# Reordering the first loads of a squared-ReLU MLP: x on one queue, w1 behind the activation table load

## The chip, the cores and the metric

The kernel runs on one NeuronCore of one Trainium2 chip. The metric is the device time of one execution in microseconds (us); the time before is the median of nine runs.

The engines are named as in the profile: PE is TensorE's matmul, PEld its weight load, DVE is VectorE, ACT is ScalarE, POOL is GpSimd, SP is SyncE. SPq and ACTq are the instruction queues of SyncE and ScalarE, from which loads are issued.

## The reference

```python
B, S, D, F = 1, 2048, 576, 4608          # x, w1, b1, w2, b2 all bfloat16

h = jnp.einsum("bsd,df->bsf", x, w1) + b1
zero = jnp.zeros_like(h)
r = jnp.where(h > zero, h, zero)
h = r * r
out = jnp.einsum("bsf,fd->bsd", h, w2) + b2
```

Two matrix products with a squared ReLU between them: 2048 rows, 576 columns in, 4608 hidden, 576 out.

## The kernel before

The 2048 rows are worked on in four blocks of 512. For each block the kernel forms h transposed (hidden units on partitions, rows along the free axis): ScalarE applies ReLU with the bias (L169), VectorE squares (L170), and the second product reads the result (L253 and L272). All of w1 and w2 is loaded once and stays in SBUF.

The first product needs x transposed. For blocks 1 to 3 a transposing DMA delivers it. For block 0 [...]the block is loaded plainly as four x tiles of 128 rows (`load_x`, L72), transposed by TensorE against an identity (`x_transpose`, L146, five 128x128 transposes per tile) and copied out of PSUM by VectorE (L151, L153) and ScalarE (L152) in two halves of 256 rows (`x_copies`). Afterwards VectorE makes a second arrangement of the same data (`dup_windows`, L115 and L116).

The first 512 hidden units of block 0 are computed in the order "k outer": `part(h, k)` does four matmuls of 256 rows (L217) with the k-th chunk of 128 rows of w1 (`w1n`, four chunks, `load_w1n`, L76). The order is k = 0 to 3 for the first half of the rows, then k = 0 to 3 for the second, with the bias transposed in between (`make_b1T`, L159). A last pair of matmuls (L196, L198) uses the remaining 64 rows of w1, which are loaded twice, into the upper and the lower half of the partitions (`w1n8`, `load_w1n8`, L79). Then `a_rows` goes through the rest of w1 (`w1_h`, `w_h` in the profile, L82) in blocks of two times nine matmuls (L181, L183).

While the first loads are on their way TensorE runs warm-up matmuls on a constant (`WARM`, L63). ScalarE needs its activation table before its first activation; a dummy activation (L97, into a tile of its own) brings that load in early.

Order: nearly every operation is wrapped in `keep`, which holds it in program order on its engine. The loads are split by hand: SyncE issues x tiles 0 and 2, w1n chunks 0 and 2, then w1n8 and all of w1_h; ScalarE issues x tiles 1 and 3 and w1n chunks 1 and 3, then runs the table load and the dummy activation, then issues the b1 load (L98). In the compiled program eight completion semaphores are handed out to the loads in turn, so a load also waits until the load that had its semaphore eight loads before has landed.

```python
WARM = [512] * 6 + [256]
...
load_x(nc.sync, 0)
load_x(nc.scalar, 1)
load_x(nc.sync, 2)
load_x(nc.scalar, 3)
for k in range(NK):
    load_w1n(nc.sync if k % 2 == 0 else nc.scalar, k, k + 1)
```

Of the kernel before, what the change touches and what calls it, by code (L numbers as in the profile page):

```python
# [9 lines left out]
ACT = mybir.ActivationFunctionType  # L10
ALU = mybir.AluOpType
BF16 = mybir.dt.bfloat16
FP32 = mybir.dt.float32
# [4 lines left out]
def kernel(  # L18
# [9 lines left out]
    nc = tc.nc  # L28
    keep = tc.keep_in_program_order
    P = 128  # L30
# [5 lines left out]
    NFT = F // P  # L36
# [8 lines left out]
    RT = SB // P  # L45
# [3 lines left out]
    const = ctx.enter_context(tc.tile_pool(name="const", bufs=1))  # L49
# [8 lines left out]

    wps = ps_h.tile([P, 512], FP32, name="wps", tag="ph")
    ones = nc.const_aps.tensor(1.0, [P, 512], BF16)  # L60
    WARM = [512] * 6 + [256]
    for i, n in enumerate(WARM):
        keep(nc.tensor.matmul(wps[:, 0:n], lhsT=ones[:, 0:P], rhs=ones[:, 0:n], start=True, stop=True))  # L63

    xs = const.tile([P, RT, D], BF16, name="x_sb")
    w1n = wpool.tile([P, NK, GW], BF16, name="w1n")
# [4 lines left out]
    def load_x(eng, rt):  # L71
        keep(eng.dma_start(out=xs[:, rt, :], in_=x2[rt * P:(rt + 1) * P, :]))  # L72

    def load_w1n(eng, k0, k1):
        src = w1[k0 * P:k1 * P, 0:GW].rearrange("(k p) f -> p k f", p=P)
        keep(eng.dma_start(out=w1n[:, k0:k1, :], in_=src))  # L76

    def load_w1n8(eng, h):
        keep(eng.dma_start(out=w1n8[h * H:(h + 1) * H, :], in_=w1[NK * P:D, 0:GW]))  # L79
# [5 lines left out]
    b1_rows = const.tile([P, P], BF16, name="b1_rows")  # L85
    nc.vector.memset(b1_rows[:], 0.0)
    load_x(nc.sync, 0)
    load_x(nc.scalar, 1)
    load_x(nc.sync, 2)
    load_x(nc.scalar, 3)  # L90
    for k in range(NK):
        load_w1n(nc.sync if k % 2 == 0 else nc.scalar, k, k + 1)

    ident = const.tile([P, P], BF16, name="ident")
    make_identity(nc, ident[:])
    warm = const.tile([P, 1], FP32, name="warm")
    keep(nc.scalar.activation(out=warm[:], in_=nc.const_aps.tensor(0.0, [P, 1], FP32), func=ACT.Relu))  # L97
    keep(nc.scalar.dma_start(out=b1_rows[0:NFT, :], in_=b1.rearrange("(ft p) -> ft p", p=P)))  # L98
    for h in range(2):
        load_w1n8(nc.sync, h)  # L100

    E3, O, SPC, E = 0, 1, 5, 6
    LO_W = [O, O + 1, O + 2, O + 3, E, E + 1, E + 2, E3, SPC]
# [240 lines left out]
```

## Time and profile before

| | |
|---|---|
| median of 9 runs | 291.16 us (290.58 to 291.32) |
| profiled execution | 291.12 us, span of its instructions 289.4 us |
| PE busy | 284.8 us (98% of the span), 2027 matmuls |
| DVE busy | 78.6 us (27%) |
| ACT busy | 96.5 us (33%) |
| DMA | 16.59 MB, mean 57 GB/s |

The table reads as follows: TensorE is busy nearly all the time, the other engines a third of it or less, and the DMA engines are busy only in the first quarter of the span. The span runs from the first to the last instruction; the execution's time has 1.7 us around it. Of the start-up the timeline has these numbers: the loads begin to be issued at 0.73 us, the table load starts at 2.61 and takes 1.28, the first transpose starts at 3.58, the first L217 matmul at 6.01.

### The profile page before, as it was taken

How to read it: one execution, taken by the hardware profiler on the slowest of the kernel's cores; microseconds unless marked ns; L12 is line 12 of the kernel's file. 1: busy time of each engine (PE TensorE's matmuls, PEld its weight loads, DVE VectorE, ACT ScalarE, POOL GpSimd, SP SyncE). 2: the span in 40 equal slices, each digit the busy share in tenths (PEclk: the TensorE clock that was granted, in tenths of full speed). 3: DMA queues.
4: the chain of work that ended last, by engine and by line, in shares of the span. 5: the costliest groups of instructions: out<-in, count | busy, mean ns of one | idle time of the engine just before them, and what ended most of it. 6: DMA issues, size and time to landing. Idle time of an engine off the chain costs nothing.

```text
span 289.4 us, 4690 instructions
## 1 busy us (share of the span) xinstructions
PE 284.8 (98%) x2027; PEld 139.2 (48%) x2032; DVE 78.6 (27%) x177; ACT 96.5 (33%) x152; POOL 0.9 (0%) x7
## 2 busy tenths in 40 slices
PE   7999999999999999999999999999999999999996
PEld 4544444444444555555544444444444455555555
DVE  3444554444500200000015444444440001100001
ACT  3566666666500000000027666666670000000000
POOL 0000000000000000000000000000000000000000
PEclk9999999999999999999999999999999999999999
DMA  6999999300001200000000000000000110000000
GB/s 198 233 239 194 315 388 217 78 0 2 0 17 25 49 16 18 16 16 18 16 16 2 1 2 0 2 0 2 0 2 0 36 39 16 16 16 19 31 17 18
DMA packets 31573, 16.59 MB, mean 57 GB/s; under 512 B 15552, under 2 KB 31552, under 8 KB 31552
## 3 DMA queue, kind: packets, MB, share of 16 engines
q1 hardware_dynamic: 30928, 15.72, 21.8%
q10 hardware_dynamic: 624, 0.57, 0.7%
q8 instruction: 16, 0.26, 0.4%
q14 instruction: 5, 0.04, 0.0%
HBM read 11.43 MB, written 2.36 MB: 48 GB/s over the span
## 4 chain that ended last, share of the span: by engine, by line
PE 98%; DVE 0%; issue 0%
PE ph L181 42%; PE po L272 38%; PE pt L253 11%; PE pn L202 4%; PE pn L217 1%; PE wps L63 1%; PE ph L183 1%; PE pn L196 1%; PE tb L146 1%; DVE xTw L151 0%; DVE o_sb L274 0%; DVE xTw L153 0%; PE b1T_ps L159 0%; PE pn L198 0%
## 5 line engine op out<-in xcount | busy, mean ns | idle before, releaser
L183 PE MATMUL ph<-xTw,w_h 64*128 64x512 bf16 x576 | 124.6, 376 | 0.0
L181 PE MATMUL ph<-xTw,w_h 64*128 64x512 bf16 x576 | 124.6, 376 | 0.0
L272 PE MATMUL po<-w_sb,hT 128*128 128x448 bf16 (+2 forms) x612 | 109.4, 341 | 0.0
L169 ACT ACTIVATE r<-ph,b1T 128x512 bf16<-128x512 f32 x128 | 81.1, 685 | 41.6 <-PE ph L183 41.6
L181 PEld LDWEIGHTS <-w_h 64*128 64x128 bf16 x576 | 54.1, 94 | 68.3
L272 PEld LDWEIGHTS <-hT 128*128 128x128 bf16 x612 | 58.5, 98 | 51.0
L170 DVE TENSOR_TENSOR hT<-r 128x512 bf16<-128x512 bf16 x144 | 61.2, 426 | 76.9 <-ACT r L169 76.6
L183 PEld LDWEIGHTS <-w_h 64*128 64x128 bf16 x576 | 54.1, 94 | 0.0
L274 DVE TENSOR_TENSOR o_sb<-po,b_bc 128x448 bf16<-128x448 f32 (+2 forms) x17 | 10.2, 598 | 125.8 <-PE po L272 125.8
L253 PE MATMUL pt<-hT,w_sb 128*128 128x512 bf16 x142 | 31.3, 379 | 0.1
L169 ACT ACTIVATE r<-pn,b1T 128x512 bf16<-128x512 f32 x16 | 10.3, 688 | 62.7 <-PE pn L198 61.3
L253 PEld LDWEIGHTS <-w_sb 128*128 128x128 bf16 x144 | 14.1, 98 | 17.0
L256 ACT ACTIVATE oT<-pt,b2T 128x512 bf16<-128x512 f32 x4 | 2.7, 687 | 28.3 <-PE pt L253 28.3
L202 PE MATMUL pn<-xTw,w1n 128*128 128x512 bf16 x45 | 10.4, 379 | 0.4 <-issue 0.3
L202 PEld LDWEIGHTS <-w1n 128*128 128x128 bf16 x48 | 4.5, 98 | 6.0 <-issue 0.8
L217 PE MATMUL pn<-xTw,w1n 128*128 128x256 bf16 x32 | 3.7, 273 | 0.7 <-DVE xTw L153 0.7
L63 PE MATMUL wps<-const-bfloat16-1.0 128*128 128x512 bf16 (+1 forms) x7 | 2.9, 597 | 0.8 <-PEq L328 0.8
L217 PEld LDWEIGHTS <-w1n 128*128 128x128 bf16 x32 | 3.0, 98 | 1.2 <-DMA w1n<-in_w_dram 0.8
L115 DVE COPY xTw<-xTw 64x2048 bf16<-64x2048 bf16 x4 | 2.8, 690 | 0.5 <-ACT xTw L152 0.4
L116 DVE COPY xTw<-xTw 64x2048 bf16<-64x2048 bf16 x4 | 2.8, 688 | 0.1
L198 PE MATMUL pn<-xTw,w1n 64*128 64x512 bf16 x8 | 2.4, 379 | 0.0
L196 PE MATMUL pn<-xTw,w1n 64*128 64x512 bf16 x8 | 2.4, 379 | 0.0
(21 smaller groups left out, 11.1 us busy)
## 6 DMA issues: line engine op xcount, KB each, us to landing
w_sb<-in_w_dram SPq DMA_DIRECT2D x2, 2592.0 KB, 15.0
w_h<-in_w_dram SPq DMA_DIRECT2D x14, 288.0 KB, 6.8
out_dram<-o_sb SPq DMA_DIRECT2D x15, 112.0 KB, 1.7
w_h<-in_w_dram SPq DMA_DIRECT2D x4, 144.0 KB, 3.2
out_dram<-ot SPq DMA_DIRECT2D x4, 128.0 KB, 2.0
x_sb<-in_x_dram ACTq DMA_DIRECT2D x2, 144.0 KB, 2.9
x_sb<-in_x_dram SPq DMA_DIRECT2D x2, 144.0 KB, 2.8
w1n<-in_w_dram ACTq DMA_DIRECT2D x2, 128.0 KB, 3.9
```

The source lines that it names most:

```text
L63: keep(nc.tensor.matmul(wps[:, 0:n], lhsT=ones[:, 0:P], rhs=ones[:, 0:n], start=True, stop=True))
L146: keep(nc.tensor.transpose(tb[h][bank][:, slot, q * P:(q + 1) * P], xs[:, j, c0:c0 + P], ident[:]))
L169: keep(nc.scalar.activation(out=r[:], in_=bank[:], func=ACT.Relu, bias=b1T[:, ft:ft + 1], scale=1.0))
L170: keep(nc.vector.tensor_tensor(out=hTs[sb][:, ft, :], in0=r[:], in1=r[:], op=ALU.mult))
L181: keep(nc.tensor.matmul(bx[:], lhsT=w1_h[0:H, LO_C[i], jc], rhs=xT[0:H, LO_W[i], :], start=(i == 0), stop=(i == NC - 1)))
L183: keep(nc.tensor.matmul(by[:], lhsT=w1_h[H:P, UP_C[i], jc], rhs=xT[H:P, UP_W[i], :], start=(i == 0), stop=(i == NC - 1)))
L196: keep(nc.tensor.matmul(banks[2 * i][:], lhsT=w1n8[0:H, 2 * i * P:(2 * i + 1) * P], rhs=xT[0:H, SPC, :], start=start, stop=stop, skip_grou ...
L202: keep(nc.tensor.matmul(banks[g][:], lhsT=w1n[:, k, g * P:(g + 1) * P], rhs=xT[:, O + k, :], start=start, stop=stop))
L217: keep(nc.tensor.matmul(banks[g][:, hc], lhsT=w1n[:, k, g * P:(g + 1) * P], rhs=xT[:, O + k, hc], start=(h == 0 and k == 0), stop=False, s ...
L253: keep(nc.tensor.matmul(pt[:], lhsT=w2_sb[:, ft, DM:D], rhs=hT[:, ft, :], start=(i == 0), stop=(i == NFT - 1)))
L272: keep(nc.tensor.matmul(po[:, 0:d1 - d0], lhsT=hT[:, ft, jj * P:(jj + 1) * P], rhs=w2_sb[:, ft, d0:d1], start=(i == 0), stop=(i == NFT - 1)))
L274: keep(nc.vector.tensor_tensor(out=o_sb[:, d0:d1], in0=po[:, 0:d1 - d0], in1=b2_bc[:, d0:d1], op=ALU.add))
```

## The change

Five edits, all in the start-up:

1. The warm-up has 5 x 512 + 384 = 2944 columns instead of 6 x 512 + 256 = 3328.
2. All four x tiles are issued by SyncE, in order 0, 1, 2, 3.
3. The dummy activation moves to the head of ScalarE's queue. It no longer writes a tile of its own but the first column of w1n chunk 0, so the load of that chunk, which overwrites this column, has to wait until the activation has ended. The b1 load follows it on ScalarE's queue.
4. The w1n chunks swap queues: 0 and 2 on ScalarE, 1 and 3 on SyncE behind the x tiles.
5. The two w1n8 loads move from SyncE to ScalarE, behind its w1n chunks. ScalarE's L152 copies (L150 in the changed file) come after them in its queue.

In the compiled order of the changed kernel ScalarE has: table load, activation, b1 load (waits for VectorE's memset), w1n chunk 0 (waits for the activation), w1n chunk 2, first w1n8 half (waits for x tile 1 to land), second w1n8 half (waits for b1 to land), the two copies. SyncE has: x tiles 0 to 3, w1n chunk 1, w1n chunk 3 (waits for x tile 0 to land), then w1_h, of which the first waits for x tile 2, the second for x tile 3, the third for w1n chunk 0. The other engines' orders are unchanged, but for one warm-up matmul less.

```diff
-    WARM = [512] * 6 + [256]
+    WARM = [512] * 5 + [384]
...
     load_x(nc.sync, 0)
-    load_x(nc.scalar, 1)
-    load_x(nc.sync, 2)
-    load_x(nc.scalar, 3)
+    keep(nc.scalar.activation(out=w1n[:, 0, 0:1], in_=nc.const_aps.tensor(0.0, [P, 1], FP32), func=ACT.Relu))
+    keep(nc.scalar.dma_start(out=b1_rows[0:NFT, :], in_=b1.rearrange("(ft p) -> ft p", p=P)))
+    for rt in range(1, RT):
+        load_x(nc.sync, rt)
     for k in range(NK):
-        load_w1n(nc.sync if k % 2 == 0 else nc.scalar, k, k + 1)
+        load_w1n(nc.scalar if k % 2 == 0 else nc.sync, k, k + 1)
+    for h in range(2):
+        load_w1n8(nc.scalar, h)
 
     ident = const.tile([P, P], BF16, name="ident")
     make_identity(nc, ident[:])
-    warm = const.tile([P, 1], FP32, name="warm")
-    keep(nc.scalar.activation(out=warm[:], in_=nc.const_aps.tensor(0.0, [P, 1], FP32), func=ACT.Relu))
-    keep(nc.scalar.dma_start(out=b1_rows[0:NFT, :], in_=b1.rearrange("(ft p) -> ft p", p=P)))
-    for h in range(2):
-        load_w1n8(nc.sync, h)
```

## The prediction

> **What bounds the kernel now.** I read the page first, then the waits of TensorE (PE), then the chain of work over the first microseconds, then the transfers one by one. The page's chain says where the span goes:
>
> ```profile
> PE 98%; DVE 0%; issue 0%
> ```
>
> PE's own waits over the whole span are three lines, and its weight loads' waits five, of which these two are for transfers:
>
> ```profile
> PE wps L63 <- PEq L328: 0.8, 1, 0.8
> PE pn L217 <- DVE xTw L153: 0.7, 1, 0.7
> PE pn L202 <- issue: 0.3, 2, 0.2
> ...
> PEld L217 <- DMA w1n<-in_w_dram: 0.8, 1, 0.8
> PEld L146 <- DMA x_sb<-in_x_dram: 0.8, 2, 0.6
> ```
>
> The reader is to see that all that PE loses to loading lies in the start-up. From the first L217 matmul on, PE is fed to the end. So an edit of the start-up is worth exactly the move of that matmul, as long as nothing behind it runs dry. The chain of the first microseconds (start, length, what):
>
> ```profile
> 0.77 2.93 PE wps L63 x7
> 3.71 0.89 PE tb L146 x10
> 4.62 0.63 PE tb L146 x8
> ...
> 6.01 2.36 PE pn L217 x20
> ```
>
> The first L217 matmul starts at 6.01. PE's wait before it is named DVE (the chain puts L151 and L153 of the second half of x there), but those feed later matmuls; the first needs only the first L151 copy, and its weight load waits for w1n. The entries for that chunk's load on SyncE (start 1.68) and for the loads and the table load on ScalarE:
>
> ```profile
> DMA to landing us min/median/max: 4.3/4.3/4.3
> ...
> 2.61 1.28 ACT L97 ACT_TABLE_LOAD   x1 [2.61 <-issue]
> 3.90 0.20 ACT L97 ACTIVATE warm<-const-float32-0.0 128x1 f32<-128x1 f32 x1
> 4.65 0.56 ACTq L98 DMA_DIRECT2D b_rows<-in_b_dram  x1
> ```
>
> 1.68 + 4.3 = 6.0: chunk 0 of w1n lands just when PE starts. In the same way chunk 1 (ScalarE, 1.64 + 3.7) lands at 5.3, chunk 3 (2.1 + 4.2) at 6.3 and chunk 2 (2.16 + 4.3) at 6.5; x tiles 0 and 1 at 3.5 and 3.3, tile 3 at 4.4, and tile 2 at 4.6, when PE's second batch of transposes starts. Why so late is in the stretches (busy times, then clock, DMA share, GB/s):
>
> ```profile
> 1.60:2.00 0.40, 0.40 (x2) 0.13 (x1) 0.00 (x0) 0.00 (x0) 0.00 (x0) 1.00 0.55 60
> 2.00:2.40 0.40, 0.40 (x2) 0.15 (x1) 0.00 (x0) 0.00 (x0) 0.00 (x0) 1.00 0.74 196
> 2.40:5.20 2.80, 2.78 (x24) 1.71 (x22) 0.68 (x3) 1.49 (x2) 0.00 (x0) 1.00 1.04 338
> ```
>
> From 2.4 to 5.2 the DMA engines are full (share 1.04) at 338 GB/s. Start-up is bound by bytes and by their order, not by issue.
>
> **The change part by part.**
>
> *Bytes.* Four x tiles of 147 KB and four w1n chunks of 131 KB are 1.11 MB before and after. About 0.10 MB has moved by 2.4 (60 and 196 GB/s for 0.4 us each), the other 1.01 MB takes 3.0 us: 5.4, and the last chunk lands about 1 us later (6.5). No reordering moves that last landing. [...] The row agrees on bandwidth (338 GB/s shared by both), but what PE waits for is the first chunk, which landed third of four. L217 runs 20 matmuls in 2.36 us, 0.118 each, so a chunk's four take 0.47, and chunks 1, 2, 3 are needed 0.47, 0.94 and 1.42 after chunk 0. Even with the last at 6.5, PE could start at 5.1 if the last is chunk 3. I take the row: order can give up to 0.9 us.
>
> *x on SyncE alone.* Tiles 0 to 3 are issued 0.42 to 0.44 us apart from 0.73, tile 3 at about 2.1 where it was at 1.2. Alone on the engines, tile 0 is through by about 2.7 and lands at about 3.1 (3.5 before), tiles 1 and 2 follow by 0.44 each (3.5, 3.9 to 4.1). Tile 3 depends on what ScalarE's queue has in flight then.
>
> *Warm-up.* 3328 columns become 2944. Six matmuls start 0.43 apart, so 384 columns are 0.32 us: transposes may start at 3.25 instead of 3.57. Alone this is worth nothing, tile 2 and w1n come later; it only avoids delaying tile 0.
>
> *ScalarE.* The table load moves from 2.61 to 0.73 and ends at about 2.0, the ACTIVATE (now into w1n, which the load of chunk 0 overwrites) at 2.22. The compiled order has the b1 load next, waiting only for the memset (ends 0.93), then chunk 0, waiting for the ACTIVATE, chunk 2, and the two w1n8 halves; the first waits for x tile 1, the second for b1 (completion semaphores are reused after eight loads); behind these are the two L152 copies. Whether b1 is issued while the table load runs is not in the trace. Bounds: at 0.97, then chunk 0 at 2.3; or at 2.25 for 0.56, then chunk 0 at 2.85. I take the first, because nothing that b1 itself waits for is later, and keep both. [...] In the row the ACTIVATE starts 0.01 us behind the load. [...]
>
> *w1n.* ScalarE's first traffic came 1.1 us after its first issue (0.73 to about 1.8), so chunk 0 flows from 3.4, when SyncE's x tile 3 is still to come and tile 2 partly. The queues shared evenly before (tiles 0 and 1 landed 0.2 apart), so chunk 0 takes (2 x 131)/338 = 0.78 us, to 4.2; x tile 3 is through at 4.3 to 4.5 and lands at 4.7 to 4.9. Chunks 1 (SyncE) and 2 (ScalarE) share the next 0.78 us, to about 5.2, and land 0.4 to 0.9 later, as the landings before did: 5.6 to 6.1. Chunk 3 (SyncE, whose semaphore waits for x tile 0, long landed) is through by 5.7 and lands by 6.5.
> PE's first L217 matmul is then the latest of: transposes (tile 3 at 4.8, five at about 0.08: 5.2); chunk 0 (4.7 to 5.1); chunk 1 less 0.47 (5.1 to 5.6); chunk 2 less 0.94 (4.7 to 5.2); chunk 3 less 1.42 (5.1). I take 5.5, chunk 1's upper part, because before the last of a pair's landings came at the late end. With b1 behind the table load (chunk 0 at 2.85) x is clear of w1, tile 3 lands at 4.4, and the same sum gives 5.1 to 5.3.
>
> *What must not become late.* L152 copies: the second w1n8 issue ends at about 4.7 (5.5 with b1 late), the copies at 5.3 and 5.9 (6.1 and 6.7); needed at 6.4 and about 8.5. The dup copies (2 x 0.69) end by 7.4 (8.1), the pair needs them 3.66 after the start, 9.2. w1n8 lands by 7 to 7.5, also needed at 9.2. SyncE's queue is one issue shorter, with the w1n8 halves (0.57 each) gone and tiles 1 and 3 (0.43 each) come: the first w_h waits for x tile 2 and goes at about 4.1 instead of 4.63, later ones keep that lead of 0.3 to 0.6. The tightest w_h was issued at 8.05 and landed 5.2 later, 13.3, for a block that starts at about 14.0; both shift together, so its cover of 0.7 holds. Cost of all these: nothing.
>
> *Sum.* 6.01 - 5.5 = 0.5 us less. The profiled execution took 291.12 us (span 289.4), 0.04 below the median of 291.16. So span 288.9, execution 290.62, median about 290.65, or -0.18%. What a measurement of this kernel can tell from no change is 0.2%, 0.58 us.
>
> **The rivals.**
>
> *More is gained.* b1 waits behind the table load, or landings have the short tail of the x tiles (0.4): PE starts at 5.1 to 5.3, right behind the transposes, time 290.35 (290.2 to 290.5). For it: SyncE alone can keep the engines full. Against: nothing shows a stall of ScalarE's queue behind a table load.
>
> *Slower: the TensorE clock is released later.* The transposes show the step: those of 3.6 to 3.9, then those of 4.6 to 5.1,
>
> ```profile
> L146 PE MATMUL tb<-ident,x_sb x4: 289/314/314, 3.6 to 3.9; 128*128 128x128 bf16 x4
> L146 PE MATMUL tb<-ident,x_sb x10: 219/219/229, 4.6 to 5.1; 128*128 128x128 bf16 x10
> ```
>
> so full speed came at about 4.2, after 3.4 us in which PE had no gap. [...] With the shorter warm-up, gaps of 0.1 to 0.3 us open wherever an x tile lands after 3.25, 3.7 or 4.1. [...] Net of the 0.5: +0.65 to +0.75, median 291.8. It decides as soon as the release is later than about 6.5. Against: x tile 0 should land before 3.25[...].
>
> *Nothing is gained.* Sharing with chunk 0 makes tile 3 land at 5.4, or chunk 1 lands at 6.5[...]: start at 5.9 to 6.5, time 291.05 to 291.65. For it: chunk 0 landed 0.6 after chunk 1 before, though issued together.
>
> **How the numbers follow.** Main case (start 5.3 to 5.8, 290.45 to 290.95) 0.50, of which 0.12 lies below 290.58, that is over 0.2% faster. More gained: 0.27, all faster. Clock slips: 0.14, all slower. Nothing gained: 0.09, of which 0.06 within 0.2% and 0.03 slower. Faster 0.39, within 0.2% 0.44, slower 0.17. The likeliest case gives 290.65, its own range 290.45 to 290.95. The range 290.0 to 291.8 takes in the gain if every landing is early (start 4.9) and reaches the middle of the clock case.
>
> **What would show it.** Right: table load at 0.73; chunk 0's issue at about 2.3 on ScalarE; x tile 0 landing by 3.25; last transposes ending near 5.2; first L217 at 5.5 with its weight load or the second chunk's waiting for w1n; no new wait of PE after it. Wrong: transposes of 314 ns after 4.5, L217 matmuls 0.2 us apart (clock);[...] x tile 3 landing after 5.2 (sharing); PE waiting for L152 or w_h.

## The result, and the profile after

The changed kernel is slower: 291.66 us median (17 runs, 291.31 to 293.34) against 291.01 for the kernel before on the same chips (51 runs), ratio 1.0032, 95% interval 1.0024 to 1.0041. Eleven of the 17 lie within 291.31 to 291.71, three at 293.1 to 293.3; none of the 51 runs before is above 291.64. The forecast was 290.65. Here and below the ratio follows the means of the runs (291.91 against 290.97 here), so it includes the runs near 293, and it leaves out three executions in a slow state: 434.89 us in experiment 4, 303.66 in experiment 7 (its profiled one, at a granted clock of 0.95) and 378.45 of the kernel before.

The profiled execution took 291.71 us (span 289.9). Its chain is no longer TensorE (PE) alone; the page's shares of the span:

```profile
PE 87%; SPq 8%; DMA 3%; issue 1%; DVE 0%
```

The waits of the weight loads (us in total, times, longest) have lost w1n and gained w_h:

```profile
PEld L144 <- DMA x_sb<-in_x_dram: 1.6, 3, 0.8
...
PEld L181 <- DMA w_h<-in_w_dram: 1.1, 2, 0.5
```

TensorE's start-up, as the timeline has it (start, length, idle before and what ended it):

```profile
3.18 1.27 PE L144 MATMUL tb<-ident,x_sb 128*128 128x128 bf16 x10
4.98 0.45 PE L144 MATMUL tb<-ident,x_sb 128*128 128x128 bf16 x5 [0.53 <-DMA x_sb<-in_x_dram]
5.65 0.45 PE L144 MATMUL tb<-ident,x_sb 128*128 128x128 bf16 x5 [0.22 <-DMA x_sb<-in_x_dram]
5.96 2.34 PE L215 MATMUL pn<-xTw,w1n 128*128 128x256 bf16 x20
```

x tile 0 is early as planned, but tiles 2 and 3 come at 4.95 and 5.6, later than the 4.6 and 4.4 of before. The first matmul on w1n (now L215) starts at 5.96 instead of 6.01: nearly nothing gained. The first matmul on w_h starts at 10.04 instead of 10.11. From there to the end of the span it is 279.9 us, where it was 279.3, so in this pair of profiles all of the loss lies behind the start-up. There PE loses time twice, as the chain shows for the second loss (start, length):

```profile
28.91 5.05 DMA w_h<-in_w_dram
34.00 0.39 PE ph L181
```

Both waits are for pieces of w1_h. The other one ends at 14.35: that piece was issued at 8.44 and landed 5.9 later (8.05 and 5.2 before). By the last block of the first stage PE is 0.59 us late (its matmuls start at 73.61, before at 73.02), and stays so to the end.

What had changed for w_h is in the stretches 10 to 18 us (w_h, with a transposing load issued at 17.73 before) and 36 to 44 us (w2), beside 2.4 to 4.0 us (start-up loads). The last two columns are the DMA share and GB/s. Before, then after:

```profile
2.40:4.00 1.60, 1.60 (x9) 0.73 (x8) 0.00 (x0) 1.38 (x2) 0.00 (x0) 1.00 1.04 340
10.00:18.00 8.00, 8.00 (x78) 3.60 (x74) 4.26 (x10) 6.12 (x10) 0.00 (x0) 1.00 1.21 244
36.00:44.00 8.00, 8.00 (x78) 3.60 (x75) 4.07 (x10) 5.29 (x10) 0.00 (x0) 1.00 1.08 388
```

```profile
2.40:4.00 1.60, 1.60 (x11) 1.07 (x10) 0.00 (x0) 0.00 (x0) 0.00 (x0) 1.00 0.94 236
10.00:18.00 8.00, 7.95 (x73) 3.42 (x71) 4.23 (x10) 6.11 (x10) 0.00 (x0) 1.00 1.22 201
36.00:44.00 8.00, 8.00 (x78) 3.62 (x76) 4.23 (x10) 5.30 (x9) 0.23 (x1) 1.00 1.09 345
```

The engines are as full as before in the last two stretches (1.22 and 1.09), but move 18% and 11% less. These loads are issued in the same order from the same queue in both kernels. What differs is their destination. The change dropped the dummy activation's own tile, which took 32 bytes per partition, and everything allocated behind it moved by as much. In the compiled program w1n, w1_h (the tile of w_h) and w2 start at multiples of 256 bytes of a partition before, and 32 bytes short of one after.

### The profile page after: what moved, and what is told of

It reads as the page before. It is cut to its first block, busy times and chain, and to the rows that moved or that the text cites. A ratio compares the mean times of both kernels' runs of the same rounds, so it can differ in the third digit from the quotient of the medians.

```text
span 289.9 us, 4688 instructions
## 1 busy us (share of the span) xinstructions
PE 285.2 (98%) x2026; PEld 139.2 (48%) x2031; DVE 78.6 (27%) x177; ACT 96.6 (33%) x152; POOL 0.9 (0%) x7
## 4 chain that ended last, share of the span: by engine, by line
PE 87%; SPq 8%; DMA 3%; issue 1%; DVE 0%
PE po L270 38%; PE ph L179 21%; PE ph L181 14%; PE pt L251 11%; SPq L82 5%; PE pn L200 4%; SPq L120 2%; DMA w_h<-in_w_dram 2%; DMA x_sb<-in_x_dram 1%; SPq L121 0%; PE pn L194 0%; SPq L72 0%; PE pn L196 0%; DVE o_sb L272 0%
## 5 line engine op out<-in xcount | busy, mean ns | idle before, releaser
L215 PE MATMUL pn<-xTw,w1n 128*128 128x256 bf16 x32 | 3.7, 272 | 0.0
L215 PEld LDWEIGHTS <-w1n 128*128 128x128 bf16 x32 | 3.0, 98 | 0.3
L144 PE MATMUL tb<-ident,x_sb 128*128 128x128 bf16 x20 | 2.2, 268 | 0.7 <-DMA x_sb<-in_x_dram 0.7
L144 PEld LDWEIGHTS <-x_sb 128*128 128x128 bf16 x20 | 1.7, 121 | 1.7 <-DMA x_sb<-in_x_dram 1.6
```

The lines of the kernel that those rows point to most:

```text
L144: keep(nc.tensor.transpose(tb[h][bank][:, slot, q * P:(q + 1) * P], xs[:, j, c0:c0 + P], ident[:]))
L215: keep(nc.tensor.matmul(banks[g][:, hc], lhsT=w1n[:, k, g * P:(g + 1) * P], rhs=xT[:, O + k, hc], start=(h == 0 and k == 0), stop=False, s ...
```

## The experiments

All ratios are to the kernel before, run on the same chip.

**1. Is it the addresses or the queues?** The changed kernel with the 32 bytes set aside again:

```diff
     make_identity(nc, ident[:])
+    pad = const.tile([P, 1], FP32, name="pad")
```

> The changed kernel, with 32 bytes of SBUF per partition set aside where the dummy activation's own tile lay before, so that w1n, w1_h, w2 and the tiles behind them have their old addresses (multiples of 256) again. Address theory (the change removed a 32-byte tile, everything behind it moved by 32 bytes, and loads into such addresses are slower): w_h moves at about 240 GB/s between 10 and 25 us instead of 198, PE no longer waits for w_h, ratio to the kernel before 0.9995 to 1.000 (the first L215 matmul still starts at 5.9 to 6.0). Queue theory (the first w_h is issued 0.3 us later because its completion semaphore waits for x tile 2, and all of w_h lands late behind it): addresses do nothing, w_h at about 200 GB/s, PE waits about 0.6 us for w_h, ratio 1.003.

Measured: 291.16 us, ratio 1.0013 (1.0002 to 1.0023). Its stretches:

```profile
2.40:4.00 1.60, 1.60 (x11) 0.95 (x10) 0.00 (x0) 0.00 (x0) 0.00 (x0) 1.00 1.00 249
10.00:18.00 8.00, 8.00 (x78) 3.62 (x76) 4.26 (x10) 6.13 (x11) 0.00 (x0) 1.00 1.17 254
36.00:44.00 8.00, 8.00 (x78) 3.60 (x74) 4.05 (x10) 5.30 (x9) 0.00 (x0) 1.00 1.08 387
```

The rates of w_h and w2 are back and no wait for w_h is left. More than half of the loss is gone, not all: two of 22 runs were at 293.08 (without them the mean is 0.06% above the kernel before), and the order of the queues, with good addresses, is still no gain.

**2. The other half of the same test.** The kernel before with the addresses of the changed one:

```diff
     warm = const.tile([P, 1], FP32, name="warm")
+    pad = const.tile([P, 1], FP32, name="pad")
```

> The kernel before, with 32 bytes of SBUF per partition set aside behind the dummy activation's tile: the queues are those of before, the addresses of w1n, w1_h, w2 and what follows are 32 bytes off a multiple of 256, as in the changed kernel. Address theory: w_h at about 200 GB/s between 10 and 25 us instead of 240, the tightest w_h lands about 0.7 us later than 13.3 and eats its cover, so PE waits 0 to 0.6 us; ratio 1.001 to 1.003, with single runs up to 2 us slower. Queue theory: w_h at 240, ratio 1.000.

Measured: 291.46 us, ratio 1.0022 (1.0014 to 1.0029). One extra tile that nobody uses makes the median 0.6 us longer:

```profile
10.00:18.00 8.00, 8.00 (x78) 3.61 (x74) 4.25 (x10) 6.10 (x10) 0.00 (x0) 1.00 1.18 204
36.00:44.00 8.00, 8.00 (x76) 3.60 (x74) 4.02 (x10) 5.29 (x10) 0.36 (x1) 1.00 1.08 349
```

and PE waits for w_h:

```profile
PEld L184 <- DMA w_h<-in_w_dram: 0.4, 1, 0.4
```

The two halves, 0.22% for the addresses and 0.13% for the rest, come to 0.35%, against the 0.32% measured; each is known to about 0.1%. The medians do not add up (0.62 and 0.32 us, against 0.65). They need not: a PE that starts later has less to wait for a load that lands at a fixed time, though no run tests that alone.

**3. Which multiple counts.** The same with 64 and 128 bytes:

```diff
+    pad = const.tile([P, 16], FP32, name="pad")     # 64 bytes; 32 elements for 128 bytes
```

> The kernel before, with 64 bytes set aside at the same place. Address theory, unit of 64 bytes: as before, w_h at 240 GB/s, ratio 1.000. Address theory, unit of 256 bytes: w_h at about 200, ratio 1.001 to 1.003, as with 32. Queue theory: ratio 1.000 with w_h at 240 in all of these kernels.

> The kernel before, with 128 bytes set aside at the same place. Address theory, unit of 64 or 128 bytes: as before, w_h at 240 GB/s, ratio 1.000. Unit of 256 bytes: w_h at about 200, ratio 1.001 to 1.003. Queue theory: ratio 1.000, w_h at 240.

Measured: 64 bytes 291.43 us, ratio 1.0019 (1.0011 to 1.0026); 128 bytes 290.88 us, ratio 1.0001 (0.9992 to 1.0009). The w2 stretch for 64, then both stretches for 128:

```profile
36.00:44.00 8.00, 8.00 (x78) 3.60 (x74) 4.57 (x10) 5.23 (x9) 0.18 (x1) 1.00 1.08 344
```

```profile
10.00:18.00 8.00, 8.00 (x78) 3.69 (x74) 4.25 (x10) 6.12 (x11) 0.00 (x0) 1.00 1.19 230
36.00:44.00 8.00, 8.00 (x78) 3.62 (x76) 4.04 (x10) 5.29 (x10) 0.00 (x0) 1.00 1.08 387
```

Of the shifts tried, 32 and 64 bytes cost time and 128 does not. Whether 128 bytes are free for the load itself is less clear. Rows of w2 are 1152 bytes, so half of them already start 128 bytes off a multiple of 256 before, and w2 cannot tell. The rows of w_h, most of them 512 bytes long, can. With w1_h 128 bytes off they came at 230 GB/s here and at 227 in experiment 9, below the 244 to 268 of the eight profiles on a multiple of 256, but nobody waited for them here. For w_h 32 and 64 bytes cost more than 128 (204 and 216 GB/s against 230); the cause of the loss inside the DMA path was not shown and stays open.

**4. Why x tiles 2 and 3 are late.** With the old addresses, all w1n chunks on SyncE:

```diff
-        load_w1n(nc.scalar if k % 2 == 0 else nc.sync, k, k + 1)
+        load_w1n(nc.sync, k, k + 1)
```

> The changed kernel with the old addresses (as in the first experiment), and with all four w1n chunks on SyncE behind the x tiles, so that nothing but b1 and later w1n8 is on ScalarE's queue. Two reasons for x tile 3's late landing (5.4 to 5.6 in the changed kernel) are told apart. Sharing theory (w1n chunk 0 on the other queue takes half of the engines from 3.8 on): tile 3 lands at 4.3 to 4.4, the chunks behind it at about 4.8, 5.3, 5.8, 6.2, the first matmul on w1n starts at 4.8 to 5.0, 0.7 earlier than in the first experiment, ratio 0.997 to 0.998 of the kernel before. Single-queue theory (one queue alone carries 250 to 280 GB/s where two carry 350 to 380): tile 3 lands at 4.6 or later, the last chunk at 6.8 or later, the first matmul at 5.3 to 5.6, ratio 0.999 to 1.001.

Measured: 291.55 us, ratio 1.0037 (1.0017 to 1.0057), three of eight runs near 293. The test was not clean: the w1n8 loads, now behind b1 alone on ScalarE's queue, went out at 1.62 and 2.16 and took their share. Still, the sharing theory's gain did not come. The start-up row is again that of x on one queue:

```profile
2.40:4.00 1.60, 1.60 (x11) 1.07 (x10) 0.00 (x0) 0.00 (x0) 0.00 (x0) 1.00 0.87 240
```

Over all profiles but that of experiment 7 the same stretch has 338 to 364 GB/s in the nine kernels with x on two queues and 210 to 249 in the six with x on SyncE alone. That need not be the number of queues. SyncE issues an x tile every 0.4 to 0.5 us, so by 2.4 us five of the eight x and w1n loads had been issued in the changed kernel and all eight in the kernel before; the two were not separated. The profile of experiment 4 caught one of the executions near 293 (292.92 us):

```profile
5.44 1.25 PE L145 MATMUL tb<-ident,x_sb 128*128 128x128 bf16 x10 [0.99 <-DMA x_sb<-in_x_dram]
6.48 3.69 PE L216 MATMUL pn<-xTw,w1n 128*128 128x256 bf16 x20
```

20 matmuls take 3.69 us instead of 2.34, after a gap of 0.99 us for x tile 2: until about 9.2 TensorE works at about half speed (matmuls of 256 columns start 0.21 us apart instead of 0.11). The granted clock of these stretches reads 1.00 all the same, so this step shows in the durations only; that it is a step of TensorE's clock is my reading of them, not shown.

**5. One part of the change alone: w1n chunks swap queues.**

```diff
-        load_w1n(nc.sync if k % 2 == 0 else nc.scalar, k, k + 1)
+        load_w1n(nc.scalar if k % 2 == 0 else nc.sync, k, k + 1)
```

> The kernel before, with one part of the change alone: w1n chunks 0 and 2 on ScalarE's queue and 1 and 3 on SyncE's; addresses, x tiles, warm-up and w1n8 as before. Order theory (what counts is which chunk lands first, as the prediction said): chunk 0 lands at 5.3 where it landed at 6.0, chunk 1 at 6.0 is needed 0.47 later; the first matmul starts at 5.5, 0.5 earlier, ratio 0.998. Rival (the landing of a chunk varies by half a microsecond from run to run and the start is not bound by it): ratio 1.000.

Measured: 290.93 us, ratio 1.0003 (0.9995 to 1.0011): no gain. In its profile the first matmul started at 5.54, as the order theory said, but that is not below what the old queues give either: in the six profiles with the old queues and warm-up (before, and the address experiments) it started at 6.01, 5.65, 5.74, 5.78, 5.55 and 5.17, at 5.65 on average. The 6.01 that the prediction took as its base was the latest of the six. The five profiles with the new queues (the changed kernel and experiments 1, 6, 10 and 13) have 5.96, 5.68, 5.88, 5.87 and 5.88, at 5.85 on average.

**6 and 7. Longer and shorter warm-up**, both in the changed kernel with the old addresses:

```diff
-    WARM = [512] * 5 + [384]
+    WARM = [512] * 6 + [256]      # 3328 columns; in the other [512] * 4, 2048 columns
```

> The changed kernel with the old addresses and the old warm-up of 3328 columns, which ends 0.32 us later. Clock theory (the single runs at 293.1 of the changed kernel, 2 of 22 in the first experiment and 3 of 17 before[...]): no run above 292, median as in the first experiment (291.0 to 291.2). Rival (those runs come from late loads of w1 or w2): 1 to 3 runs above 292.5 as there.

> The changed kernel with the old addresses and a warm-up of 2048 columns, which ends 0.75 us earlier, so that TensorE idles before x tile 0 lands. Clock theory: [...]transposes of 314 ns after 5 us and matmuls of 256 rows 0.21 us apart; ratio 1.003 to 1.008. Rival (late loads make the slow runs): distribution as in the first experiment, ratio 1.000 to 1.001.

Measured: 3328 columns 291.31 us, ratio 1.0018 (1.0007 to 1.0029), two of 21 runs at 293.2 and 293.3; 2048 columns 292.84 us, ratio 1.0061 (1.0041 to 1.0082), six runs. The first went against the clock theory as I had put it (the runs near 293 are those in which TensorE reaches full speed later, and the longer warm-up would leave none): with the longer warm-up there are still runs above 293. The second agrees with it. The warm-up bridges only the time to x tile 0: with 3328 columns tile 2 landed at 4.77, and the weight loads still waited twice for x, up to 0.3 us.

**8 and 9. Which tile's address costs.** The kernel before, w1_h alone off by 32 bytes, and everything but w1_h:

```diff
+    pad_a = wpool.tile([P, 8], FP32, name="pad_a")      # 9: 24 elements, and a pad of 32 bytes in const
     w1_h = wpool.tile([P, NC, FH], BF16, name="w1_h")
+    pad_b = wpool.tile([P, 24], FP32, name="pad_b")     # 9: 8 elements
```

> The kernel before, with w1_h alone moved to addresses 32 bytes off a multiple of 128; w1n, w2, xT and hT stay on multiples of 128. If the lost time is PE waiting for w_h, the whole cost of the 32-byte shift is here: ratio 1.002, w_h at about 205 GB/s between 10 and 18 us, PE waiting once or twice for w_h, w2 at 386 GB/s between 35 and 45. Rival (it is the start-up loads, or the engines' reads of the shifted operands): ratio 1.000.

> The complement: w1n, w1n8, w2, xT and hT moved by 32 bytes off a multiple of 128, w1_h on a multiple of 128. If the lost time is PE waiting for w_h: ratio 1.000 to 1.0005, w_h at about 245 GB/s, w2 at about 333 between 35 and 45 without anybody waiting for it. Rival: ratio 1.002.

Measured: w1_h alone 291.64 us, ratio 1.0028 (1.0017 to 1.0039); all but w1_h 291.23 us, ratio 1.0011 (1.0002 to 1.0020). With w1_h alone:

```profile
10.00:18.00 8.00, 8.00 (x77) 4.50 (x73) 4.25 (x10) 6.12 (x11) 0.00 (x0) 1.00 1.18 201
```

```profile
PEld L185 <- DMA w_h<-in_w_dram: 1.2, 2, 0.9
```

So the lost time is PE waiting for w_h: moving this one tile costs as much as moving all. The complement slows w2 (359 GB/s in 36 to 44 us), which nobody waits for. Its 0.11% is above what I expected, with an interval that nearly reaches zero. Its profile does have a wait for w_h:

```profile
PEld L186 <- DMA w_h<-in_w_dram: 0.5, 1, 0.5
```

There the sixth w_h took 5.2 us to land, as in the kernel before. But PE's first matmul on w1n had started at 5.17, 0.84 earlier than in the profile before, and PE came to that block before the load had landed. An early start can thus use up the cover of a load; whether this makes up the 0.11% stays open.

**10 and 11. Closing the gap.** Two matmuls of 384 columns between the transposes of x tiles 1 and 2, in the changed kernel with the old addresses; one of 512 in the kernel of experiment 5:

```diff
                 x_copies(0)
+                fill = ps_o.tile([P, 512], FP32, name="fill", tag="po")
+                for n in [384, 384]:
+                    keep(nc.tensor.matmul(fill[:, 0:n], lhsT=ones[:, 0:P], rhs=ones[:, 0:n], start=True, stop=True))
```

> The changed kernel with the old addresses and two matmuls of 384 columns on a constant (0.64 us at half clock) between the transposes of x tile 1 and of x tile 2, where TensorE waited 0.4 to 1.0 us for tile 2; the result is not used. Clock theory[...]: no run above 292 out of about 20, ratio 1.000 to 1.0015, median 290.9 to 291.2. Rival (the slow runs come from something else, late loads for example): still one run in ten near 293, as with both warm-ups.

> The kernel before with the w1n chunks' queues swapped (as in the fifth experiment) and one matmul of 512 columns on a constant between the transposes of x tiles 1 and 2. If the spread of 0.8 us between runs of the kernel before is the moment at which the clock is released, a start-up without gaps should release it earlier on average: ratio 0.998 to 0.9995. If the release falls where it will: ratio 1.000.

Measured: 291.16 us, ratio 1.0006 (0.9997 to 1.0014), highest of 13 runs 291.47; and 291.10 us, ratio 1.0002 (0.9994 to 1.0010). The first is as the clock theory has it, and no loss is clear of the noise any more. The second says that the spread of the kernel before is not to be had this way: no version found here beats it.

**12 and 13. The clock by itself, and in the changed kernel.** The kernel before with `WARM = [512] * 4`, all loads and addresses untouched; and the changed kernel as it is, with the two filling matmuls of experiment 10.

> The kernel before with a warm-up of 2048 columns instead of 3328, so that TensorE idles about 1.1 us before x tile 0 lands at 3.5; all loads and addresses as before. Clock theory[...]: a good part of the runs 1 to 2.5 us slower, near 292 to 293.5, ratio 1.002 to 1.008, and no w_h wait. Rival (late loads make the slow runs of the changed kernel): nothing changes, since x and w1n are what PE waits for: ratio 1.000, no run above 291.8.

> The changed kernel as it is (addresses 32 bytes off), with the two matmuls of 384 columns on a constant between the transposes of x tiles 1 and 2. Clock theory: the runs at 293 go, no run above 292.5 of about 15, while the cost of the addresses stays: median 291.4 to 291.7, ratio 1.002 to 1.003. Rival (late loads into the shifted addresses make the runs at 293): still about one run in six near 293.

Measured: the first 291.63 us, ratio 1.0027 (1.0013 to 1.0040), four of 11 runs between 291.9 and 292.65, where none of the 16 beside them is above 291.35. Its profile has the gap of 0.85 us and the step of the clock, the matmuls of 256 columns by their duration (min, median, max) and place:

```profile
3.49 2.31 PE L146 MATMUL tb<-ident,x_sb 128*128 128x128 bf16 x20 [0.85 <-DMA x_sb<-in_x_dram]
```

```profile
L217 PE MATMUL pn<-xTw,w1n x7: 421/421/421, 5.6 to 6.9; 128*128 128x256 bf16 x7
L217 PE MATMUL pn<-xTw,w1n x7: 331/421/421, 6.7 to 7.9; 128*128 128x256 bf16 x7
L217 PE MATMUL pn<-xTw,w1n x10: 272/273/421, 7.7 to 8.9; 128*128 128x256 bf16 x10
```

Full speed comes at about 8, where the profile before had it at 4.2. The moment varies without such a gap too: in the other profiles of this kernel and its address variants it lies between about 3.5 (128 bytes) and 6.4 (32 bytes). The two profiles with a gap of 0.85 us or more have it at 8 and 9.2, the latest of all read. With the slower runs, that shows that a gap costs time here with no load changed; how long a gap must be is not shown. The second: 292.02 us, ratio 1.0036 (1.0022 to 1.0049), six runs, none above 292.28, though the median is above what I expected. With the gap filled no run of 19 (experiments 10 and 13) reached 292.5; without it 7 of 60 (the changed kernel, experiments 1 and 6) were above 293. That fits, but chance alone would give zero of 19 about one time in ten.

## Why the prediction was wrong

The direction was wrong; 291.66 lies inside the range, near its end, only because the range was wide; that it is close to the 291.8 of the clock rival is coincidence. By the prediction's own steps:

- *"Cost of all these: nothing" (What must not become late).* This is the step that failed. The tightest w_h was said to keep its cover of 0.7 us because "both shift together". Its issue did not move ahead but back, from 8.05 to 8.44, since the first w_h waits for x tile 2 (4.95, not 4.1). And its transfer took 5.9 us instead of 5.2, because of its address: with the same order of the queues and the old addresses (experiments 1, 6 and 10) it took 4.8 to 5.1, was issued at 8.0 to 8.3, and PE did not wait for w_h. It landed at 14.3 instead of 13.3, and PE waited. The sum never asked where the tiles lie after one is dropped; that term is 0.22% (experiment 2), 0.6 us. Two smaller slips stand beside it. SyncE's queue has not "one issue" less: two w1n8 halves went and two x tiles came. And w_h does not shift with PE's start, as experiment 9 shows.
- *x on SyncE alone, "tiles 1 and 2 follow by 0.44 each".* The 338 GB/s of the row belong to loads issued from two queues. With x on one, 236 were moved between 2.4 and 4.0 us, at a DMA share of 0.94 (340 and 1.04 before). x tile 2 landed at 4.95 instead of 3.9 to 4.1, tile 3 at 5.6 instead of 4.7 to 4.9; in the five other profiles with this order of x (experiments 1, 4, 6, 10 and 13) tile 2 landed at 4.1 to 5.4 and tile 3 at 5.3 to 5.7. Whether this is the number of queues or only the time of issuing, the rates (338 to 364 GB/s with two, 210 to 249 with one) do not decide, because the issue time differed too, and it was not small: one x tile took 0.40 to 0.43 us to issue, and its bytes take 0.44 at 338 GB/s.
- *The first w1n matmul at 5.5.* It came at 5.96, and at 5.85 on average over five profiles. The base of 6.01 was itself one execution at the late end; the average of six is 5.65. So with the new order the start was about 0.2 us later on average, where the sum had 0.5 earlier. The spread inside each group (5.17 to 6.01, 5.68 to 5.96) is as large, so only the missing gain is clear.
- *ScalarE.* Right: table load at 0.73, b1 issued at 0.96 while it ran, ACTIVATE at 2.03, 0.02 us behind the end of the load, chunk 0 at 2.26:

```profile
0.73 1.28 ACT L88 ACT_TABLE_LOAD   x1 [0.73 <-PEq L326]
0.96 0.62 ACTq L89 DMA_DIRECT2D b_rows<-in_b_dram  x1
2.03 0.20 ACT L88 ACTIVATE w1n<-const-float32-0.0 128x1 bf16<-128x1 f32 x1
2.26 0.84 ACTq L76 DMA_DIRECT2D w1n<-in_w_dram  x2
```

- *The clock rival.* A late step to full speed is real (at about 9.2 and 8 in the profiles of experiments 4 and 12, at 4.2 in the kernel before). In the one execution near 293 with a profile the gap was the one before x tile 2, among the landings that the rival had named, but longer (0.99 us, not 0.1 to 0.3). The rival's 291.8 was my estimate: how far a gap puts off full speed was not shown. Such a step probably makes single runs 2 us slower (those near 293); it is not the reason for the median. These runs are part of the ratio: without the three runs near 293 the mean of the changed kernel is 0.23% above the kernel before, not 0.32%.

That the addresses cost about two thirds of the ratio's loss is shown by experiments 1, 2 and 8. Of the 0.13% that experiment 1 leaves, its two runs at 293.08 make about half, and with the gap filled (experiment 10) 0.06% are left, within the noise. That the late clock makes the runs near 293 is likely, not shown: one profile shows it, and the filled gap could have met none by chance. A start 0.2 us later (0.07%) would fit what remains; it rests on averages of a few profiles and is not shown either. Why x tiles and w1n chunks land up to about a microsecond apart from one execution to the next stays open.

## What to carry to other kernels

Before costing an edit of a tile list, look at where the compiled program puts the tiles behind it: here dropping 32 bytes cost 0.6 us, more than the 0.5 that the reordering was to bring, and a 32-byte pad gave more than half of the loss back. Take the rate of a queue from a stretch in which it was alone, and the base of a start-up from several executions rather than one. When a prefetched stream has as little cover as w_h had here (0.7 us), treat it as part of the path: it need not come earlier because its reader does (in experiment 9 PE started 0.84 us earlier and waited 0.5 us for w_h).

## What the runs showed of the hardware that was not expected

Loads into SBUF at addresses 32 or 64 bytes off a multiple of 128 ran at 344 to 359 GB/s (w2) and 201 to 216 (w_h). At multiples of 128 w2 ran at 374 to 391 (the 374 in the kernel with w1_h alone shifted), and w_h at 244 to 268 on a multiple of 256 and at 227 and 230 at 128 off one. The DMA engines are shown about equally full in all of these (shares of 1.08 to 1.09 and 1.14 to 1.22). The b1 load of the changed kernel, behind the dummy activation on ScalarE's queue, was issued at 0.96, while the table load ran (to 2.01) and before the activation (2.03). With the x tiles issued from one queue the start-up moved 210 to 249 GB/s between 2.4 and 4.0 us, from two 338 to 364 (queue or issue time, not separated). And TensorE's full speed, which came at 4.2 us in the profile before and between 3.5 and 6.4 in its address variants, came at about 8 in one with a gap of 0.85 us before it (experiment 12).
